# The second layer 23 pairs behind the first in place of 11, weights converted every third slot: attention and two gated layers on one core

## The chip, the cores and the metric

The kernel runs on one core of a Trainium2 chip. The metric is device time in microseconds (us) of one execution. Engines are named as the profile names them: PE (TensorE, matmuls), DVE (VectorE), ACT (ScalarE), POOL (GpSimd), SP (SyncE, which only issues DMAs).

## What is computed

The reference pools `kv` over 4x4 patches, projects it with `w_sr` to 768 keys that are values too, lets 12288 queries of width 128 attend to them, and sends the result through two layers (128 to 2048 to 128), each with an activation of its own:

```python
kv_flat = kv.reshape(B, H // 4, 4, W // 4, 4, C).mean(axis=(2, 4)).reshape(B, -1, C) @ w_sr
s = (q @ kv_flat.transpose(0, 2, 1)) / np.sqrt(C)
a = np.exp(s - s.max(-1, keepdims=True)); a /= a.sum(-1, keepdims=True) + 1e-09
x = a @ kv_flat
h = x @ moe_w_in                      # layer 1
x = (h * np.clip(h + 3.0, 0.0, 6.0) / 6.0) @ moe_w_out
h = x @ moe2_w_in                     # layer 2, beta = 1
g = np.where(h >= 1, h, np.where(h <= -1, 0.0, (h + 1) ** 2 / 4))
out = g @ moe2_w_out
```

## The kernel before, in words

All matrices are float32. To keep their accuracy a matrix is held as a high and a low part, and a product is made of three matmuls (high x high, high x low, low x high). The 12288 rows are cut into 24 blocks of 512. The 2048 hidden columns of a layer are cut into 16 pieces of 128, and two pieces make a **pair**. So each layer has 24 x 8 = 192 pairs, and pair `s` belongs to block `s // 8`.

The program is written out in **slots**, `T = 0, 1, 2, ...`, and each engine executes what it is given strictly in the order of the text, waiting where data or a buffer is not there. In slot `T` the function `slot` writes down pair `s1 = T` of layer 1 and pair `s2 = T - O2` of layer 2. O2 is the lag. So slots 0 to O2-1 have layer 1 alone, slots O2 to 191 have both layers, and slots 192 to 191+O2 have layer 2 alone.

What a pair does:

- **m_in** (L457): six matmuls of 512 columns into two tiles `h` of PSUM. There are four such tiles for both layers.
- Layer 1: `relu1` on ACT (L498, twice), `mul1` on DVE (L504, twice), then `hi_lo`: the high part on ACT (L532, twice), the low part on POOL (L533, twice).
- Layer 2: `clip2` on DVE (L511), `sq2` on ACT (L517), `max2` on DVE (L521), each twice, and `hi_lo` a slot later.
- **m_out** (L473): six matmuls that add the pair to `acc[m]`, one bank of PSUM for each layer. Layer 1's stand one slot later, layer 2's two slots later (`LAG2`), or three from slot `NS + LAG3_AT` on, where NS is 192. Layer 2's m_out stands last in a slot.
- After the eighth pair of a block layer 1's `acc[0]` is split into `x2h` (ACT, L480) and `x2l` (DVE, L481), the input of layer 2. Layer 2's `acc[1]` is transposed by DVE (`o_T`, L489) and stored. As there is one `acc[1]`, the first m_out of the next block waits for that transposition.

Attention for the next blocks lies between these. Four score tiles a block (`s_mm`, L364, six matmuls of 384 columns) are followed by the maximum on DVE (L375) and the exponential on ACT (L400). One slot later comes the tail: the sum's reciprocal on DVE (L408, L411), the product on ACT (L414, only while `T < ACT_T`), the low part on DVE (L421), and a transposing DMA. Twice a block `av` (L436, 18 matmuls of 256 columns) makes `xh` (ACT, L441) and `xl` (DVE, L442). From slot 4 on the score tiles stand in even slots and the tails in odd ones; in slots 0 to 4 every slot has scores. Queries are transposed by `q_T` (DVE L338, ACT L339, POOL L340).

The weights are **converted** when loaded, in 16 pieces `j0` to `j15` of 512 columns. A piece takes four steps, one a slot: step 0 is two ACT instructions (L163, L165); step 1 is two DVE instructions (L172, L174) and an addition on POOL (L176); step 2 is one DVE instruction (L181); step 3 is the high part on ACT (L192) and the low part on POOL (L194). They stand last but for the m_outs in a slot. Pieces 0 to 6 are begun ahead of slot 0; the slots in which 7 to 15 begin are listed in `CONV_AT`. A raw piece waits in a tile that another purpose leaves free (`stage`), and `LOADS` is the order of the loads.

Of the kernel before, what the change touches and what calls it, by code (L numbers as in the profile page):

```python
# [8 lines left out]
FP32 = mybir.dt.float32  # L9
F32R = mybir.dt.float32r  # L10
# [6 lines left out]
AX = mybir.AxisListType  # L17

W_MIN = 3.4332275390625e-05
O2, LAG2 = 11, 2  # L20

LOADS = "w k0 k1 w k4 k6 k2 k5 k3 w q0 k8 k7 k9 k10 k11 w w w w w q1 w w w w w w q2 w w"
KV_MODE = "DDVVPPPPPPPP"
PROLOGUE = """
j0.0 j0.1 k0 j1.0 k1 j0.2 k2 k3 g2 k4 g3 j1.1 t1 k5 j2.0 j0.3 p1 q0 k6 z1 t2 j2.1 p2 t0
# [3 lines left out]
j4.3 x1 j6.1 j5.3  # L32
"""
SPLIT0 = (0, 2)
CONV_AT = (0, 1, 4, 6, 7, 8, 10, 12, 14)
ACT_T = 32
LAG3_AT = 5
EARLY = (0, 1, 2, 3, 5, 7, 4, 6, 8, 10, 9, 13, 2)
EB = 3
AB = 3  # L40
SPLIT_AT = (5, 7, 9)
LO_DVE = ((0, 'out', 2),)
KV_ACT = (0, 1, 2, 3)

# [2 lines left out]
def tile_attn_moe_moe2(  # L47
# [18 lines left out]
    BLK = 512  # L66
# [9 lines left out]
    hl_p = ctx.enter_context(tc.tile_pool(name="hl", bufs=2))  # L76
    q_p = ctx.enter_context(tc.tile_pool(name="q", bufs=2))
    x_p = ctx.enter_context(tc.tile_pool(name="x", bufs=2))
    e_p = ctx.enter_context(tc.tile_pool(name="e", bufs=EB))
    a_p = ctx.enter_context(tc.tile_pool(name="a", bufs=AB))  # L80
    at_p = ctx.enter_context(tc.tile_pool(name="at", bufs=2))
# [18 lines left out]
    def f32(t):  # L100
        return t.bitcast(FP32)
# [4 lines left out]
    def new_h():  # L106
        return ps_h.tile([128, 512], FP32, tag="h", name="h")
# [76 lines left out]
    def w_stage3(job):  # L184
# [244 lines left out]
    def av(b, i, early=False):  # L429
        at = at_t.pop((b, i))  # L430
        ah, al = at[:, :KC], at[:, KC:]
        ps = (new_h() if early else new_s()[:, 0])[:, :BLK // 2]
        n = 0
        for k in range(KC):
            for l, r in ((vv[0], ah), (vv[0], al), (vv[1], ah)):
                nc.tensor.matmul(ps, l[:, k, :], r[:, k, :], start=(n == 0), stop=(n == 3 * KC - 1))  # L436
                n += 1
        if i == 0:
            x_t[b] = [x_p.tile([128, BLK], F32R, tag=f"x{p}", name=f"x{p}") for p in "hl"]
        hi, lo = (t[:, i * 256:(i + 1) * 256] for t in x_t[b])  # L440
# [19 lines left out]
    def m_out(m, s):  # L460
        b, c = divmod(s, NPAIR)
        assert (m, "out", c // 2) in ready
        if c == 0:
            acc[m] = ps_a.tile([128, BLK], FP32, tag=f"acc{m}", name=f"acc{m}")
        hi, lo = hl_t.pop((m, s))
        wh, wl = w_out[m]
        order = [(k, n) for k in range(2) for n in range(3)]
        if (m, s) == (1, NS - 1):
            order = [(0, 0), (0, 2), (1, 0), (1, 2), (0, 1), (1, 1)]
        for i, (k, n) in enumerate(order):  # L470
            ws = slice((2 * c + k) * 128, (2 * c + k + 1) * 128)
            l, r = ((wh, hi), (wh, lo), (wl, hi))[n]
            nc.tensor.matmul(  # L473
                acc[m], l[:, ws], r[:, k, :], start=(c == 0 and i == 0), stop=(c == NPAIR - 1 and i == 5)
            )
        if c == NPAIR - 1:
            if m == 0:
                hi = x_p.tile([128, BLK], F32R, tag="x2h", name="x2h")
                lo = x_p.tile([128, BLK], F32R, tag="x2l", name="x2l")
                nc.scalar.copy(out=hi, in_=acc[0])  # L480
                nc.vector.tensor_tensor(out=lo, in0=acc[0], in1=f32(hi), op=ALU.subtract)  # L481
                x2_t[b] = (hi, lo)
            else:
                o_t[b] = acc[1]
# [22 lines left out]

    def clip2(s, k):
        if k == 0:
            g_t[1, s] = hl_p.tile([128, 2, 512], FP32, tag="g2", name="g2")  # L510
        nc.vector.tensor_scalar(  # L511
            out=g_t[1, s][:, k], in0=h_t[1, s, k], scalar1=1.0, scalar2=-1.0, op0=ALU.min, op1=ALU.max
        )
# [8 lines left out]

    def hi_lo(m, s):
        g = g_t.pop((m, s))

        n = 1 if m == 0 or (s >= NS - O2 and s % 2) else 2
        hi = hl_p.tile([128, 2, 512], F32R, tag=f"h{n}", name=f"h{n}")
        lo = hl_p.tile([128, 2, 512], F32R, tag=f"l{n}", name=f"l{n}")
        hl_t[m, s] = hi, lo
        for k in range(2):  # L530
            eng = nc.vector if s == NS - 1 else nc.gpsimd
            nc.scalar.copy(out=hi[:, k], in_=g[:, k])  # L532
            eng.tensor_tensor(out=lo[:, k], in0=g[:, k], in1=f32(hi[:, k]), op=ALU.subtract)  # L533
# [3 lines left out]
    NS = NB * NPAIR  # L537
# [4 lines left out]
    s_at, tail_at, av_at, q_at, o_at = {}, {}, {}, {}, {}  # L542
# [39 lines left out]
    def slot(T):  # L582
        s1, s2 = T, T - O2
        if ok(s1):
            for k in range(2):
                m_in(0, s1, k)
                relu1(s1, k)
        if T in tail_at:
            s_tail_a(*tail_at[T], on_act=T < ACT_T)
            if T >= ACT_T:  # L590
                s_tail_b(*tail_at[T])
        if ok(s1):
            for k in range(2):
                mul1(s1, k)
        if ok(s2):
            for k in range(2):
                m_in(1, s2, k)
                clip2(s2, k)
        if ok(s2 - 1):
            hi_lo(1, s2 - 1)  # L600
        if ok(s1):
            hi_lo(0, s1)
        if T in o_at:
            o_T(o_at[T])
        if ok(s2):
            for k in range(2):
                sq2(s2, k)
        if T in s_at:
            s_mm(*s_at[T], split=T in SPLIT_AT)
        if T in tail_at and T < ACT_T:  # L610
            s_tail_b(*tail_at[T])
        if ok(s2):
            for k in range(2):
                max2(s2, k)
        if T in s_at:
            s_exp(*s_at[T])
        if T in av_at:
            av(*av_at[T], early=T < O2)
        if T in q_at:
            q_T(q_at[T])  # L620
        conv_step(T in CONV_AT)
        load_next()
        if ok(s1 - 1):
            m_out(0, s1 - 1)
        lag = LAG2 if T < NS + LAG3_AT else 3
        if ok(out2_at[0]) and s2 - lag == out2_at[0]:
            m_out(1, out2_at[0])
            out2_at[0] += 1
# [80 lines left out]
```

## Time and profile before

| | |
|---|---|
| median of 3 runs | 1354.13 us (1353.67 to 1357.67) |
| the profiled execution | 1357.25 us; its span, first to last instruction, 1355.5 us |
| busy | PE 1313.2 us (97%), DVE 1156.6 (85%), POOL 1079.2 (80%), ACT 1033.8 (76%) |
| mean granted clock of PE | 0.988 of full speed |

The profiled execution took 3.1 us more than the median of the runs, and 1.75 us of its time lie outside the span. Times of the trace count from the span's start. The granted clock is given as a share of 2.4 GHz; 0.5 is 1.2 GHz.

### The profile page before, as it was taken

The numbers are of one execution on the slowest core, as the hardware profiler recorded it, in microseconds if no ns is written. First come the engines' busy times: TensorE is split into PE (matmuls) and PEld (weight loads), VectorE is DVE, ScalarE is ACT, GpSimd is POOL, SyncE is SP. The second block draws the span as 40 slices with busy tenths as digits, with TensorE's granted clock in tenths as the row PEclk, the third lists the DMA queues.
The fourth block names the chain that finished last, engine by engine and source line by source line (L and its number), as shares of the span: only waits on it lengthen the run. The fifth ranks groups of instructions, "written<-read, shape, count | busy, mean of one in ns | idle before, by whom it ended". The sixth has DMA issues, their size and how long they took to land.

```text
span 1355.5 us, 18465 instructions
## 1 busy us (share of the span) xinstructions
PE 1313.2 (97%) x6244; PEld 1073.5 (79%) x6244; DVE 1156.6 (85%) x1815; ACT 1033.8 (76%) x1917; POOL 1079.2 (80%) x826
## 2 busy tenths in 40 slices
PE   8587999999999999999999999999999999999998
PEld 6465788888888888888888888888888888888876
DVE  3798988898988988888989989888898899898677
ACT  2678888877777787778777777877777777777776
POOL 2478998887887887888878878878878888787887
PEclk9789999999999999999999999999999999999999
DMA  9642221221212221212212122222212122121000
GB/s 326 130 93 39 59 46 33 47 40 36 51 32 43 40 43 34 49 33 43 47 28 52 32 43 41 43 43 40 43 32 51 32 44 34 33 43 25 8 9 16
DMA packets 260783, 66.28 MB, mean 49 GB/s; under 512 B 252368, under 2 KB 256592, under 8 KB 260688
## 3 DMA queue, kind: packets, MB, share of 16 engines
q1 hardware_dynamic: 259456, 62.94, 23.8%
q10 hardware_dynamic: 1232, 2.16, 0.4%
q8 instruction: 49, 0.80, 0.2%
q14 instruction: 46, 0.38, 0.1%
HBM read 21.04 MB, written 6.29 MB: 20 GB/s over the span
## 4 chain that ended last, share of the span: by engine, by line
PE 87%; DVE 4%; POOL 1%; ACT 1%; issue 1%; DMA 0%; ACTq 0%; DVEq 0%; POOLq 0%
PE acc L473 37%; PE h L457 37%; PE s L364 7%; PE s L436 6%; POOL l L533 1%; DVE t L504 1%; DVE a L421 1%; DVE nm L375 1%; DVE wa L172 0%; ACT t L498 0%; DVE g L181 0%; DVE wa L174 0%; DMA wst<-in_moe_w_out_dram 0%; ACT a L414 0%; DVE g L511 0%
## 5 line engine op out<-in xcount | busy, mean ns | idle before, releaser
L533 POOL TENSOR_TENSOR l<-g,h 128x512 fp32r<-128x512 f32 x382 | 507.9, 1351 | 210.0 <-ACT h L532 150.6
L533 POOL TENSOR_TENSOR l<-t,h 128x512 fp32r<-128x512 f32 x382 | 501.2, 1334 | 10.5 <-ACT h L532 7.1
L498 ACT ACTIVATE t<-h 128x512 f32<-128x512 f32 x384 | 227.1, 597 | 215.8 <-PE h L457 207.8
L504 DVE SCALAR_TENSOR_TENSOR t<-t,h 128x512 f32<-128x512 f32 x384 | 248.7, 682 | 128.2 <-ACT t L498 128.2
L521 DVE TENSOR_TENSOR g<-h,g 128x512 f32<-128x512 f32 x384 | 245.6, 679 | 13.4 <-ACT g L517 6.6
L532 ACT CAST h<-t 128x512 fp32r<-128x512 f32 x384 | 225.1, 620 | 35.2 <-DVE t L504 31.9
L511 DVE TENSOR_SCALAR g<-h 128x512 f32<-128x512 f32 x384 | 245.7, 680 | 0.7 <-POOL l L533 0.4
L517 ACT ACTIVATE g<-g 128x512 f32<-128x512 f32 x384 | 228.0, 628 | 1.7 <-DVE g L511 1.7
L532 ACT CAST h<-g 128x512 fp32r<-128x512 f32 x384 | 217.7, 617 | 4.2 <-DVE g L521 3.6
L457 PE MATMUL h<-xh,wi0h 128*128 128x512 f32 x384 | 152.6, 397 | 5.9 <-ACT xh L441 4.5
L473 PE MATMUL acc<-h,wo0h 128*128 128x512 f32 x384 | 156.2, 407 | 0.0
L473 PE MATMUL acc<-l,wo0h 128*128 128x512 f32 x384 | 153.1, 399 | 2.2 <-POOL l L533 2.0
L457 PE MATMUL h<-x2h,wi1h 128*128 128x512 f32 x384 | 152.4, 397 | 2.4 <-DVE g L521 2.2
L457 PE MATMUL h<-xl,wi0h 128*128 128x512 f32 x384 | 152.7, 398 | 0.7 <-DVE xl L442 0.7
L473 PE MATMUL acc<-h,wo1h 128*128 128x512 f32 x384 | 151.9, 396 | 0.5 <-DVE o L489 0.4
L457 PE MATMUL h<-x2h,wi1l 128*128 128x512 f32 x384 | 152.2, 396 | 0.0
L457 PE MATMUL h<-xh,wi0l 128*128 128x512 f32 x384 | 152.2, 396 | 0.0
L473 PE MATMUL acc<-h,wo0l 128*128 128x512 f32 x384 | 152.2, 396 | 0.0
L457 PE MATMUL h<-x2l,wi1h 128*128 128x512 f32 x384 | 151.7, 395 | 0.0
L473 PE MATMUL acc<-h,wo1l 128*128 128x512 f32 x384 | 151.3, 394 | 0.0
L473 PE MATMUL acc<-l,wo1h 128*128 128x512 f32 x384 | 151.3, 395 | 0.0
L421 DVE SCALAR_TENSOR_TENSOR a<-e,rc,a 128x768 f16<-128x768 f32 x96 | 137.2, 1429 | 3.3 <-ACT a L414 0.5
(134 smaller groups left out, 2128.6 us busy)
## 6 DMA issues: line engine op xcount, KB each, us to landing
q<-in_q_dram SPq DMA_DIRECT2D x96, 64.0 KB, 2.4
out_dram<-o SPq DMA_DIRECT2D x96, 64.0 KB, 1.9
h<-in_kv_dram SPq DMA_DIRECT2D x4, 512.0 KB, 8.9
l<-in_moe_w_in_dram SPq DMA_DIRECT2D x3, 512.0 KB, 8.7
at<-a SPq DMA_TRANSPOSE x96, 3.7
g<-in_moe_w_in_dram SPq DMA_DIRECT2D x2, 512.0 KB, 6.8
h<-in_moe_w_out_dram SPq DMA_DIRECT2D x2, 512.0 KB, 9.5
l<-in_kv_dram ACTq DMA_DIRECT2D x2, 512.0 KB, 10.4
```

Source lines behind the costliest of these rows:

```text
L364: nc.tensor.matmul(ps[h], l[:, js], r[:, ks], start=(n == 0), stop=(n == 2))
L421: nc.vector.scalar_tensor_tensor(out=a[:, 1], in0=e, scalar=rc, in1=a[:, 0], op0=ALU.mult, op1=ALU.subtract)
L436: nc.tensor.matmul(ps, l[:, k, :], r[:, k, :], start=(n == 0), stop=(n == 3 * KC - 1))
L457: nc.tensor.matmul(ps, l[:, ws], r, start=(n == 0), stop=(n == 2))
L473: nc.tensor.matmul(acc[m], l[:, ws], r[:, k, :], start=(c == 0 and i == 0), stop=(c == NPAIR - 1 and i == 5))
L498: nc.scalar.activation(out=g_t[0, s][:, k], in_=h_t[0, s, k], func=ACTF.Relu, scale=1.0 / 6.0, bias=0.5)
L504: nc.vector.scalar_tensor_tensor(out=g, in0=g, scalar=1.0, in1=h_t.pop((0, s, k)), op0=ALU.min, op1=ALU.mult)
L511: nc.vector.tensor_scalar(out=g_t[1, s][:, k], in0=h_t[1, s, k], scalar1=1.0, scalar2=-1.0, op0=ALU.min, op1=ALU.max)
L517: nc.scalar.activation(out=g, in_=g, func=ACTF.Square, scale=0.5, bias=0.5)
L521: nc.vector.tensor_tensor(out=g, in0=h_t.pop((1, s, k)), in1=g, op=ALU.max)
L532: nc.scalar.copy(out=hi[:, k], in_=g[:, k])
L533: eng.tensor_tensor(out=lo[:, k], in0=g[:, k], in1=f32(hi[:, k]), op=ALU.subtract)
```

## The change

O2 goes from 11 to 23. `CONV_AT` spaces the nine pieces by three slots (the first by two), so that at most one piece is in its DVE steps in any slot. Block inputs `x2h`, `x2l` get three buffers in place of two. In the slots with layer 2 alone, odd pairs take `t1`'s buffers for `g` and even ones their own. `LAG3_AT` goes from 5 to 17, so that a lag of three holds for the last six pairs as before. `ACT_T` goes from 32 to 26. The load of block 2's queries stands earlier. `EARLY_AV` keeps the choice of the PSUM tile of `av` as it was.

```diff
-O2, LAG2 = 11, 2
+O2, LAG2 = 23, 2
-LOADS = "w k0 k1 w k4 k6 k2 k5 k3 w q0 k8 k7 k9 k10 k11 w w w w w q1 w w w w w w q2 w w"
+LOADS = "w k0 k1 w k4 k6 k2 k5 k3 w q0 k8 k7 k9 k10 k11 w w w w w q1 w q2 w w w w w w w"
-CONV_AT = (0, 1, 4, 6, 7, 8, 10, 12, 14)
-ACT_T = 32
-LAG3_AT = 5
+CONV_AT = (0, 2, 5, 8, 11, 14, 17, 20, 23)
+ACT_T = 26
+LAG3_AT = O2 - 6
+EARLY_AV = 11
+    x2_p = ctx.enter_context(tc.tile_pool(name="x2", bufs=3))
-                hi = x_p.tile([128, BLK], F32R, tag="x2h", name="x2h")
-                lo = x_p.tile([128, BLK], F32R, tag="x2l", name="x2l")
+                hi = x2_p.tile([128, BLK], F32R, tag="x2h", name="x2h")
+                lo = x2_p.tile([128, BLK], F32R, tag="x2l", name="x2l")
-            g_t[1, s] = hl_p.tile([128, 2, 512], FP32, tag="g2", name="g2")
+            tag = "t1" if s >= NS - O2 and s % 2 else "g2"
+            g_t[1, s] = hl_p.tile([128, 2, 512], FP32, tag=tag, name=tag)
-            av(*av_at[T], early=T < O2)
+            av(*av_at[T], early=T < EARLY_AV)
```

Lines after L78 move by two or three, so DVE's L504 is L506 in the kernel of after, L172 is L174, and so on.

**DVE in slot 9 and up to slot 10's products.** Before, these are the products `t` of slot 9, the attention tail, and then step 2 of one piece and step 1 of the next ahead of slot 10's products:

```order
L504 SCALAR_TENSOR_TENSOR t_1029<-t_1029,h 128x512 x2
L421 SCALAR_TENSOR_TENSOR a<-e,rc,a 128x768
L442 SCALAR_TENSOR_TENSOR xl<-h,csc,xh 128x256
L181 SCALAR_TENSOR_TENSOR g_554<-g_554,wa 128x512
L172 TENSOR_SCALAR wa<-wa 128x512
L174 TENSOR_SCALAR wa<-wa 128x512
L504 SCALAR_TENSOR_TENSOR t_1092<-t_1092,h 128x512 x2
```

In the kernel of after the same slot reads:

```order
L506 SCALAR_TENSOR_TENSOR t_1021<-t_1021,h 128x512 x2
L423 SCALAR_TENSOR_TENSOR a<-e,rc,a 128x768
L444 SCALAR_TENSOR_TENSOR xl<-h,csc,xh 128x256
L174 TENSOR_SCALAR wa<-wa 128x512
L176 TENSOR_SCALAR wa<-wa 128x512
L506 SCALAR_TENSOR_TENSOR t_1081<-t_1081,h 128x512 x2
```

The step 2 (L181) of the other piece has left this slot; step 1 of one piece is still there.

**DVE in slots 11 and 12.** Before, layer 2 begins here with its clips (L511) and maxima (L521):

```order
L504 SCALAR_TENSOR_TENSOR t_1147<-t_1147,h 128x512 x2
L511 TENSOR_SCALAR g_1165<-h 128x512 x2
L421 SCALAR_TENSOR_TENSOR a<-e,rc,a 128x768
L521 TENSOR_TENSOR g_1165<-h,g_1165 128x512 x2
L172 TENSOR_SCALAR wa<-wa 128x512
L174 TENSOR_SCALAR wa<-wa 128x512
L504 SCALAR_TENSOR_TENSOR t_1201<-t_1201,h 128x512 x2
```

In the kernel of after slots 11 and 12, up to the products of slot 13, have layer 1 alone:

```order
L506 SCALAR_TENSOR_TENSOR t_1130<-t_1130,h 128x512 x2
L423 SCALAR_TENSOR_TENSOR a<-e,rc,a 128x768
L506 SCALAR_TENSOR_TENSOR t_1168<-t_1168,h 128x512 x2
L377 TENSOR_REDUCE nm<-s 128x1
L174 TENSOR_SCALAR wa<-wa 128x512
L176 TENSOR_SCALAR wa<-wa 128x512
L410 TENSOR_SCALAR su<-su 128x1
L413 RECIPROCAL rc<-su 128x1
L506 SCALAR_TENSOR_TENSOR t_1208<-t_1208,h 128x512 x2
```

Layer 2's instructions have left the slot, and step 1 of a piece now stands behind the maximum of a slot with scores.

**PE at the end of a block of layer 2, in slots with layer 2 alone.** Before, this happens once, in slot 197, where the lag goes from two to three: the m_in rows of slots 197 and 198 (twelve L457, of which eleven are shown) stand ahead of the first m_out into the next `acc`:

```order
L457 MATMUL h<-x2l,wi1h 128x512
L457 MATMUL h<-x2h,wi1l 128x512
L457 MATMUL h<-x2h,wi1h 128x512
L457 MATMUL h<-x2l,wi1h 128x512
L457 MATMUL h<-x2h,wi1l 128x512
L457 MATMUL h<-x2h,wi1h 128x512
L457 MATMUL h<-x2l,wi1h 128x512
L457 MATMUL h<-x2h,wi1l 128x512
L457 MATMUL h<-x2h,wi1h 128x512
L457 MATMUL h<-x2l,wi1h 128x512
L457 MATMUL h<-x2h,wi1l 128x512
L473 MATMUL acc_13827<-h_13763,wo1h 128x512
```

In the kernel of after it happens in slots 193, 201 and 209. Slot 209 looks like the rows above. In slot 201, as in 193, six matmuls stand between the last of one `acc` and the first of the next:

```order
L475 MATMUL acc_13363<-h_13516,wo1l 128x512
L459 MATMUL h<-x2h,wi1h 128x512
L459 MATMUL h<-x2l,wi1h 128x512
L459 MATMUL h<-x2h,wi1l 128x512
L459 MATMUL h<-x2h,wi1h 128x512
L459 MATMUL h<-x2l,wi1h 128x512
L459 MATMUL h<-x2h,wi1l 128x512
L475 MATMUL acc_13586<-h_13543,wo1h 128x512
L475 MATMUL acc_13586<-l_13544,wo1h 128x512
```

On DVE the transposition of `acc_13363` stands behind the clips of those six matmuls' results:

```order
L525 TENSOR_TENSOR t_13536<-h,t_13536 128x512 x2
L515 TENSOR_SCALAR g_13563<-h 128x512 x2
L491 STREAM_TRANSPOSE o<-acc_13363 128x512
L525 TENSOR_TENSOR g_13563<-h,g_13563 128x512 x2
L515 TENSOR_SCALAR t_13597<-h 128x512 x2
```

The transposition has not moved within its slot; what moved is the slot, from one with two layers to one with layer 2 alone.

## Rows read from the trace of the kernel before

**Rows 1.** Busy time in three stretches: from slot 0, from slot 13, layer 2 alone.

```profile
60.80:139.30 78.50, 64.83 (x270) 50.30 (x271) 69.99 (x98) 60.67 (x110) 63.24 (x44) 0.89 0.39 81
139.30:1314.80 1175.50, 1174.28 (x5569) 962.94 (x5568) 1022.06 (x1600) 918.63 (x1703) 970.31 (x742) 1.00 0.21 38
1314.80:1350.30 35.50, 35.37 (x151) 27.94 (x149) 32.65 (x52) 28.07 (x47) 28.40 (x23) 1.00 0.05 9
```

**Rows 2.** PE in order of time, slots 5 and 6: start, duration, instruction.

```profile
92.38 0.39 PE L436 MATMUL h<-at,vh 128*128 128x256 f16 x2
...
94.28 0.48 PE L473 MATMUL acc<-h,wo0h 128*128 128x512 f32 x1
...
95.76 0.39 PE L457 MATMUL h<-xh,wi0h 128*128 128x512 f32 x1
...
97.17 0.34 PE L364 MATMUL s<-kTh,qh 128*128 128x384 f32 x1
...
98.22 0.39 PE L473 MATMUL acc<-h,wo0h 128*128 128x512 f32 x1
```

**Rows 3.** ACT in order of time, slots 5 and 10.

```profile
94.04 1.07 ACT L498 ACTIVATE t<-h 128x512 f32<-128x512 f32 x2
...
96.86 0.48 ACT L441 ACTIVATE xh<-h,csc 128x256 fp32r<-128x256 f32 x1
97.22 1.08 ACT L498 ACTIVATE t<-h 128x512 f32<-128x512 f32 x2
...
125.53 0.90 ACT L400 ACTIVATE e<-s,nm 128x768 f32<-128x768 f32 x1 [0.25 <-DVE nm L375]
...
126.42 0.61 ACT L339 CAST qh<-qT 128x512 fp32r<-128x512 f32 x1
...
127.48 0.66 ACT L163 ACTIVATE wa<-wst 128x512 f32<-128x512 f32 x1
...
128.60 1.06 ACT L498 ACTIVATE t<-h 128x512 f32<-128x512 f32 x2
```

**Rows 4.** DVE in order of time, end of slot 9 and slot 10.

```profile
120.47 1.51 DVE L172 TENSOR_SCALAR wa<-wa 128x512 f32<-128x512 f32 x1
...
123.36 1.27 DVE L504 SCALAR_TENSOR_TENSOR t<-t,h 128x512 f32<-128x512 f32 x2
124.55 0.94 DVE L375 TENSOR_REDUCE nm<-s 128x1 f32<-128x768 f32 x1
```

**Rows 5.** DVE groups from 62 to 142 us: count, busy us, mean ns.

```profile
L172 DVE TENSOR_SCALAR wa<-wa 128x512 f32<-128x512 f32 x8 | 9.6, 1201 | 0.0
L174 DVE TENSOR_SCALAR wa<-wa 128x512 uint32<-128x512 uint32 x8 | 7.3, 918 | 0.3
L181 DVE SCALAR_TENSOR_TENSOR l<-l,wa 128x512 uint32<-128x512 uint32 x2 | 2.5, 1257 | 0.0
```

**Rows 6.** The same groups from 30 to 52 us, ahead of slot 0.

```profile
L174 DVE TENSOR_SCALAR wa<-wa 128x512 uint32<-128x512 uint32 x2 | 0.9, 428 | 0.1
L172 DVE TENSOR_SCALAR wa<-wa 128x512 f32<-128x512 f32 x2 | 0.8, 410 | 0.0
L181 DVE SCALAR_TENSOR_TENSOR l<-l,wa 128x512 uint32<-128x512 uint32 x1 | 0.7, 693 | 0.0
```

**Rows 7.** PE in order of time, from the end of slot 197's m_in.

```profile
1331.62 0.40 PE L457 MATMUL h<-x2h,wi1h 128*128 128x512 f32 x1
...
1333.29 0.47 PE L473 MATMUL acc<-h,wo1h 128*128 128x512 f32 x1
```

**Rows 8.** DVE at the same place.

```profile
1332.43 0.70 DVE L489 STREAM_TRANSPOSE o<-acc 128x512 f32<-128x512 f32 x1
```

**Rows 9.** PE in order of time, two idle times and matmuls behind them.

```profile
107.32 0.61 PE L457 MATMUL h<-xh,wi0h 128*128 128x512 f32 x1 [2.20 <-ACT xh L441]
...
110.14 0.52 PE L364 MATMUL s<-kTh,qh 128*128 128x384 f32 x1
...
129.96 0.50 PE L457 MATMUL h<-xh,wi0h 128*128 128x512 f32 x1 [1.34 <-DVE t L504]
```

## The prediction

> **What bounds the kernel now.** I read first the busy time by stretches. The reader is to see that PE works without a gap from slot 13 on: 1174.28 of 1175.50 us, and 35.37 of 35.50 in the slots with layer 2 alone, both at full clock [rows 1]. Between the first m_in of slot 0 (60.80 us) and that of slot 13 (139.30 us) it is busy for only 64.83 of 78.50 us, at a granted clock of 0.89. The number of matmuls doesn't change, so the time can only change where PE idles or is slow: in the ramp, and wherever the change opens a new gap.
>
> How much does the ramp lose? PE in order of time at full clock gives the prices: `av` 1.90 us (92.38 to 94.28), six matmuls of m_in 1.41 (95.76 to 97.17), a score tile 1.05 (97.17 to 98.22) [rows 2]. I count 1.41 for m_out too. Up to slot 13 PE has 13 m_ins and 12 m_outs of layer 1, two m_ins of layer 2, 9 score tiles and 3 `av`: 27 x 1.41 + 9 x 1.05 + 3 x 1.90 = 53.2 us. So 78.5 - 53.2 = 25.3 us are lost. The change can gain at most that, and it puts twelve more slots with layer 1 alone in the ramp, whose own losses come out of the gain.
>
> **What sets the length of a ramp slot.** Not PE, but the chain between ACT and DVE. In a slot with scores, DVE makes the products (123.36), then the maximum (124.55); ACT starts the exponential at 125.53 [rows 3, 4] and is free for the next thing at 126.42, 3.06 us after the products began. Then comes what else ACT has: a query cast and step 3 of a piece, together 1.06 (126.42 to 127.48), step 0 1.12 (127.48 to 128.60) [rows 3], and then the next relu, 0.63 us ahead of the next products (relu pairs and product pairs are each about 1.2 us long and overlap by half). So such a slot takes 3.06 + 0.63 = 3.69 us and ACT's extras. A slot with a tail and `av` takes 3.18 us of ACT (relu at 94.04 to relu at 97.22 [rows 3]) and extras; without `av` and its cast (96.86 to 97.22) 2.82. The rule gives slot 10 of before as 123.36 - 0.63 + 3.69 + 1.06 + 1.12 = 128.60, which is where the relu of slot 11 stands.
>
> DVE adds pushes: steps 1 and 2 stand ahead of the next products. At the end of slot 9 the two instructions of step 1 took from 120.47 to 123.36, 2.89 us [rows 4], while ACT had written slot 10's relu long before. In the ramp L172 and L174 take 1.20 and 0.92 us in the mean, L181 1.26 [rows 5]; ahead of slot 0, where POOL has little to do, the first three take 0.41, 0.43 and 0.69 [rows 6]. So step 1 costs 2.1 us in the ramp against 0.84, and step 2 1.2 against 0.7. The Trainium skill ("SBUF — State Buffer", section "SBUF: two separate sides") says why: DVE and POOL share a pair of ports under an exclusive lock, and the loser waits for the other's whole instruction. The trace agrees with it (0.41 against 1.20 us), and it speaks against the change: spacing the pieces makes none of them cheaper as long as POOL is fed in every slot.
>
> **The change part by part.**
>
> *Ahead of slot 0 and slots 0 to 4: about 0.2 us gained.* On DVE and ACT the same instructions stand in the same order ahead of slot 0; the earlier query load meets an SP queue with nothing to issue. Slots 0 to 4 hold two steps 1 as before and a step 2 in slot 4. I take relu of slot 5 at 93.8 in place of 94.04.
>
> *Slots 5 to 10.* Two pieces in place of four have their steps 1 here. Slots with steps 3 and 0 (0.53 + 1.12 us of ACT): slot 5 3.18 + 1.65 = 4.9, slot 8 3.69 + 1.65 = 5.4 and 0.8 for the cast to `x2h` (0.5) and PE's wait for `xh`, which stands there today [rows 9] (0.3 of it reaches ACT, by choice), 6.2. Slots with step 1: slot 6, where DVE is free 2.78 us after relu, then 2.1 and 0.35 for the reciprocal, so the products come 0.9 late, 4.7; slot 9, where tail and `xl` last until 3.6 and step 1 until 5.7 against products due at 3.8, 5.2. Slots with step 2: slot 7 4.5, slot 10 3.69 + 0.53, 4.3 with a little push. Sum 29.8 us against 34.6 before (94.04 to 128.60 [rows 3]). Relu of slot 11 stands at 123.6, 5.0 us earlier.
>
> *Slots 11 to 22.* Scores and tails alternate, so the same rules hold. Slots 11, 14, 17, 20 with steps 3 and 0: 4.5 + 5.4 + 4.9 + 5.4 = 20.2. Slots 12, 15, 18, 21 with step 1, pushed by 1.0 to 2.0 us: 4.7 + 4.4 + 5.2 + 5.1 = 19.4 (18 has the query cast). Slots 13, 16, 19, 22 with step 2: 4.2 + 4.2 + 3.4 + 3.7 = 15.5. Sum 55.1 us, 4.6 a slot, where PE needs 24 x 1.41 + 6 x 1.05 + 3 x 1.90 = 45.8. Relu of slot 23 stands at 178.7.
>
> *Layer 2's begin.* Before, from relu of slot 11 (128.60) to m_in of slot 13 (139.30) 10.7 us pass. Slots 23 and 24 hold the same work without the step 1 that pushed slot 12's products (2.1 us), and with the copies to `x2h` and `x2l` that fall in slot 24, two of the casts' 0.53: 10.7 - 2.1 + 1.1 = 9.7. So m_in of slot 25 starts at 188.4.
>
> *Balance of the ramp: 3.3 us lost.* Up to slot 25 after, PE has 24 half slots, 6 score tiles and 3 `av` more than up to slot 13 before, 45.8 us. With no change in losses slot 25 would begin at 139.30 + 45.8 = 185.1; it begins at 188.4. Bounds: if steps 1 and 2 cost what they cost beside an idle POOL [rows 6], the pushes of slots 6 to 22 shrink by 3 x 1.0 (even slots, whole push) + 3 x 1.26 (odd) + 3 x 0.5 (step 2), 8 us, so 5 gained; if each of the six steps 1 costs 2.89 [rows 4], 5 more, so 8 lost.
>
> *The end: 3.3 us lost.* When a block of layer 2 ends, PE's next m_out waits until DVE has transposed `acc[1]`, and the transposition stands behind two clips that need this slot's m_in. Before, that happens among slots with layer 2 alone once, in slot 197, and there the lag rises to three, so that PE has m_in of slot 198 to do first. Its m_in of slot 197 ends at 1331.62, the transposition runs from 1332.43 for 0.70 us, and m_out starts at 1333.29 [rows 7, 8]. Without the m_in between, PE would have idled for 1333.29 - 1331.62 = 1.67 us. After, blocks end in slots 193, 201 and 209; only 209 has the lag of three. So two waits of 1.67 us each, 3.3. Behind them all of PE's remaining work is queued, and PE has no slack there. A bound below is nothing if DVE ran ahead of PE; it can't, as the clips need this slot's m_in.
>
> *Nothing.* The third `x2` buffer, the alternating `g` buffers and ACT_T change no instruction's length, and behind slot 26 PE covers the other engines as it does now: none is busy for more than 83% (POOL 970.31 of 1175.50 us [rows 1]). Without that cover ACT_T would put three products more on DVE, in slots 27, 29 and 31, each below 1.3 us by the rows of DVE at hand.
>
> *The clock.* Behind PE's idle time of 2.20 us at 107.32 the next m_in took until 110.14, 2.82 us in place of 1.41: the clock was at the lower level, and the score matmul at 110.14 still took 0.52 us against 0.34 at 97.17 [rows 2, 9]. Behind 1.34 us of idle time at 129.96 nothing of the kind shows. The two new waits of 1.67 us lie between. They stand in dense work, like that at 129.96, and the nearer row is 1.34, so I take nothing; a fall would cost the 1.4 us of that m_in and a little of what follows, 1.7 by choice, so up to 3.4 for both.
>
> Sum: 3.3 + 3.3 = 6.6 us slower. Against the profiled execution's 1357.25 that is 1363.9; it ran 3.1 above the median of 1354.13, so a median of **1360.7**.
>
> **The rivals.**
>
> *The ramp runs at PE's pace (faster).* If POOL, with one piece in three slots, leaves DVE the gaps it needs, the pushes vanish: slots 5 to 22 take 76.9 in place of 84.9 us and the median is 1352.7; down to PE's own 71.7 us there (25.9 and 45.8) it is 1347.5. It decides from a step 1 near 0.84 us on. For it: POOL gets fewer instructions per slot. Against it: the means of [rows 5] were taken while POOL idled for a fifth of the time (63.24 of 78.50 us busy [rows 1]). 22%, three quarters of it below 1350.
>
> *The gains and losses cancel.* The ramp gains 0 to 4, with slots that I made too long (PE may run ahead of ACT by the four `h` tiles, which smooths some pushes), the end loses 3.3: 1353.4 to 1357.4. 22%.
>
> *A low clock in the longer ramp.* Each slot of 11 to 22 leaves PE 0.8 us idle, in one piece if it waits for one instruction. If the clock falls there as at 107.32, PE itself becomes the limit: three to five falls of 1.7 us, 1365.8 to 1369.2. Against it: 0.8 is below the 1.34 that brought no fall. 12%.
>
> *Forecast, 1357 to 1365.* 44%. That the change doesn't do what it says is ruled out by the order of instructions above.
>
> **How the numbers follow.** About 0.3% (4 us) is what the runs can tell from no change, so faster is below 1350.1 and slower above 1358.2. Faster takes three quarters of the first rival, 0.17; same its rest, the second rival and the lower edge of the forecast, 0.32; slower the remainder, 0.51. The range of 1350 to 1369 leaves out 2 in 10, mostly below. The forecast's own range is 1357 to 1365.
>
> **What would show it.** The first layer 2 m_in near 180 us; slots 11 to 22 of 4.6 us each, with PE idle 0.8 a slot and its waits named after DVE's products or ACT; L172 and L174 at a mean of 2 us together; two waits of PE's m_out for the transposition, of 1.67 us, some 70 and 46 us ahead of the end (slots of 2.8 us). It is wrong if step 1 falls to 1 us, if slots 11 to 22 come near 3.9 us, or if the two waits are absent.

## The result: slower by 0.7%

The kernel of after takes 1364.72 us in the median of 4 runs (1363.41 to 1366.01), the kernel before 1354.06 us on the same chip (4 runs, 1353.67 to 1357.67). The ratio is 1.0073, with an interval of 1.0053 to 1.0092. The forecast was 1360.7 us, slower, in a range of 1350 to 1369.

A median of 4 runs of the kernel before can lie 2 to 3 us low: in later comparisons, with 17 to 35 runs, its median was 1355.97 to 1356.92 us, and after is 7.8 to 8.8 us (about 0.6%) slower than that. So I judge the steps by the two profiled executions, 1357.25 us before and 1364.46 us after: 7.2 us slower, where the sum of the prediction was 6.6.

The head of the page of after: the span and the busy time of each engine.

```profile
span 1362.6 us, 18443 instructions
...
PE 1313.9 (96%) x6244; PEld 1070.3 (79%) x6244; DVE 1160.5 (85%) x1818; ACT 1035.6 (76%) x1914; POOL 1077.3 (79%) x826
```

PE is busy for 0.7 us more than before (1313.2 us), so 6.4 of the 7.1 us of the span are idle time of PE. The busy time by stretches shows where it lies. As in [rows 1], a row gives the stretch and its length, then the busy time (and the instructions) of PE, PEld (PE's loading of weights), DVE, ACT and POOL, then the granted clock, the busy share of the DMA engines and GB/s. The stretches are slots 0 to 4, 5 to 10 and 11 to 22 (counted from relu to relu), then up to the m_in of slot 25, the long middle, and the first 49 us of the end.

```profile
61.20:91.98 30.78, 25.80 (x110) 20.36 (x110) 28.32 (x39) 23.08 (x43) 23.50 (x17) 0.89 0.45 104
91.98:123.18 31.20, 26.94 (x130) 19.79 (x129) 24.42 (x39) 24.15 (x47) 23.63 (x17) 1.00 0.41 83
123.18:179.30 56.12, 48.45 (x236) 37.88 (x236) 44.03 (x64) 45.46 (x84) 47.72 (x35) 1.00 0.28 52
179.30:188.51 9.21, 7.50 (x34) 5.77 (x33) 8.66 (x15) 9.21 (x20) 7.87 (x6) 1.00 0.22 43
188.51:1290.00 1101.49, 1099.56 (x5213) 902.40 (x5212) 962.12 (x1503) 853.12 (x1583) 900.57 (x692) 1.00 0.21 38
1290.00:1339.00 49.00, 46.00 (x197) 36.66 (x196) 44.02 (x68) 39.56 (x65) 41.25 (x33) 1.00 0.07 11
```

The m_in of slot 25 starts at 188.51. The ramp without change in losses would have had it at 185.1, so 3.4 us are lost there. The middle has 1.93 us of PE's idle time against 1.22 behind slot 13 before [rows 1], 0.7 more. The end has 3.0 us of idle time, and 0.17 us more at each of its two waits, as worked out below. These make 3.4 + 0.7 + 3.3 = 7.4 us, against 7.1 measured.

**The ramp.** PE's waits from 91 to 190 us (who was waited for, us in total, times, longest):

```profile
PE acc L475 <- POOL l L536: 7.4, 11, 1.2
...
PE h L459 <- DVE g L525: 1.7, 1, 1.7
```

PE mostly waits for POOL's low part of the products, yet POOL is busy for 47.72 of 56.12 us in slots 11 to 22 and isn't short of time. The low part is the last link. ACT and DVE in order of time at the begin of slot 16, where step 1 of a piece stands behind slot 15's tail, show the first one:

```profile
144.32 1.10 ACT L500 ACTIVATE t<-h 128x512 f32<-128x512 f32 x2
144.38 1.49 DVE L174 TENSOR_SCALAR wa<-wa 128x512 f32<-128x512 f32 x1
...
145.90 1.39 DVE L176 TENSOR_SCALAR wa<-wa 128x512 uint32<-128x512 uint32 x1
...
147.21 1.27 DVE L506 SCALAR_TENSOR_TENSOR t<-t,h 128x512 f32<-128x512 f32 x2
...
147.92 1.22 ACT L535 CAST h<-t 128x512 fp32r<-128x512 f32 x2 [2.51 <-DVE t L506]
```

The relu begins at 144.32, but DVE is in step 1 from 144.38 to 147.2, the products follow at 147.21, and ACT has idled for 2.51 us when it makes their high part. So the products were pushed by more than 2 us, and everything behind them with them. The groups of step 1 on DVE from 62 to 190 us have these means:

```profile
L176 DVE TENSOR_SCALAR wa<-wa 128x512 uint32<-128x512 uint32 x9 | 11.6, 1288 | 0.3
...
L174 DVE TENSOR_SCALAR wa<-wa 128x512 f32<-128x512 f32 x10 | 9.5, 952 | 0.0
```

Together 2.24 us, against 2.12 in the kernel before (1.20 + 0.92 [rows 5]): the first became cheaper and the second dearer, and spacing the pieces made step 1 as a whole no cheaper.

**Where layer 2 begins.** PE in order of time in slot 12 of before, from layer 2's m_in to the m_in of slot 13:

```profile
133.83 0.50 PE L457 MATMUL h<-x2h,wi1h 128*128 128x512 f32 x1 [2.23 <-DVE g L521]
...
135.24 0.63 PE L457 MATMUL h<-x2h,wi1l 128*128 128x512 f32 x1
...
139.30 0.39 PE L457 MATMUL h<-xh,wi0h 128*128 128x512 f32 x1
```

The same matmuls in slot 24 of after, up to the m_in of slot 25:

```profile
184.54 0.51 PE L459 MATMUL h<-x2h,wi1h 128*128 128x512 f32 x1 [1.71 <-DVE g L525]
...
188.51 0.40 PE L459 MATMUL h<-xh,wi0h 128*128 128x512 f32 x1
```

In between PE works without a wait in both kernels, for 5.47 us before and 3.97 after. Before, the granted clock is 0.64 from 133.5 to 138.3: behind 2.23 us of idle time it fell to the lower level (1.2 GHz), and a matmul of 512 columns is shown with 0.63 us in place of 0.39. After, it stays at 1.00 behind 1.71 us of idle time. Up to these m_ins both kernels take the same, 5.23 us from relu of slot 11 (128.60 to 133.83) and 5.24 from relu of slot 23 (179.30 to 184.54). So the 1.5 us that after gains where layer 2 begins are a fall of the clock that it doesn't have.

**The end.** DVE and PE in order of time in slot 193, the first of the two places where a block of layer 2 ends with layer 2 alone:

```profile
1290.20 1.32 DVE L515 TENSOR_SCALAR g<-h 128x512 f32<-128x512 f32 x2
...
1290.39 0.40 PE L459 MATMUL h<-x2h,wi1l 128*128 128x512 f32 x1
...
1291.44 0.71 DVE L491 STREAM_TRANSPOSE o<-acc 128x512 f32<-128x512 f32 x1
...
1292.29 0.47 PE L475 MATMUL acc<-h,wo1h 128*128 128x512 f32 x1 [1.50 <-ACT g L521]
```

The last matmul of m_in starts at 1290.39; in a dense stretch the next starts 0.23 us later, at 1290.62, but m_out starts at 1292.29, 1.67 us late, of which 1.50 are shown as idle. The second place, at 1316.43, has the same 1.50. The row names ACT's square as the releaser, which ended at about the same time as the transposition; that it is the transposition is shown by the experiment below that moves it.

### The profile page after: what moved, and what is told of

Its sections match the earlier page's. It is cut to its first block, busy times and chain, and to the rows that moved or that the text cites. A ratio compares the mean times of both kernels' runs of the same rounds, so it can differ in the third digit from the quotient of the medians.

```text
span 1362.6 us, 18443 instructions
## 1 busy us (share of the span) xinstructions
PE 1313.9 (96%) x6244; PEld 1070.3 (79%) x6244; DVE 1160.5 (85%) x1818; ACT 1035.6 (76%) x1914; POOL 1077.3 (79%) x826
## 4 chain that ended last, share of the span: by engine, by line
PE 78%; DVE 6%; ACT 3%; issue 1%; POOL 0%; DVEq 0%; ACTq 0%
PE acc L475 34%; PE h L459 33%; PE s L366 6%; PE s L438 6%; DVE g L525 1%; DVE g L515 1%; DVE t L506 1%; DVE t L525 1%; ACT g L521 1%; ACT h L535 1%; ACT t L521 0%; ACT t L500 0%; DVE t L515 0%; DVE nm L377 0%; POOL l L536 0%
## 5 line engine op out<-in xcount | busy, mean ns | idle before, releaser
L536 POOL TENSOR_TENSOR l<-g,h 128x512 fp32r<-128x512 f32 x360 | 472.0, 1332 | 204.3 <-ACT h L535 153.0
L536 POOL TENSOR_TENSOR l<-t,h 128x512 fp32r<-128x512 f32 x404 | 533.8, 1342 | 25.7 <-ACT h L535 23.3
L506 DVE SCALAR_TENSOR_TENSOR t<-t,h 128x512 f32<-128x512 f32 x384 | 248.2, 682 | 120.9 <-ACT t L500 120.7
L535 ACT CAST h<-t 128x512 fp32r<-128x512 f32 x408 | 240.0, 620 | 40.1 <-DVE t L506 33.2
L525 DVE TENSOR_TENSOR g<-h,g 128x512 f32<-128x512 f32 x360 | 230.6, 681 | 13.6 <-ACT g L521 7.1
L515 DVE TENSOR_SCALAR g<-h 128x512 f32<-128x512 f32 x360 | 230.9, 682 | 0.7
L521 ACT ACTIVATE g<-g 128x512 f32<-128x512 f32 x360 | 214.7, 629 | 1.5 <-DVE g L515 1.1
L535 ACT CAST h<-g 128x512 fp32r<-128x512 f32 x360 | 204.2, 617 | 5.2 <-DVE g L525 5.2
## 6 DMA issues: line engine op xcount, KB each, us to landing
l<-in_kv_dram ACTq DMA_DIRECT2D x2, 512.0 KB, 10.3
```

The lines of the kernel that those rows point to most:

```text
L506: nc.vector.scalar_tensor_tensor(out=g, in0=g, scalar=1.0, in1=h_t.pop((0, s, k)), op0=ALU.min, op1=ALU.mult)
L515: nc.vector.tensor_scalar(out=g_t[1, s][:, k], in0=h_t[1, s, k], scalar1=1.0, scalar2=-1.0, op0=ALU.min, op1=ALU.max)
L521: nc.scalar.activation(out=g, in_=g, func=ACTF.Square, scale=0.5, bias=0.5)
L525: nc.vector.tensor_tensor(out=g, in0=h_t.pop((1, s, k)), in1=g, op=ALU.max)
```

## The experiments

Theory: after loses about 3.3 us where step 1 and step 2 push the products in the long ramp, and 3.3 at the end behind two transpositions. Rivals: the first profile of before was not typical; the loss is the clock's; or the ramp is slow for a reason other than DVE's steps. "Before" in a ratio is always the kernel before on the same chip and in the same comparison.

### The kernel before again

> The kernel before, unchanged, for a profile of an execution nearer to its median than the one shown (1357.25 against 1354.06 us). Every theory: ratio 1.000. If the executions of before differ in the prologue or the ramp, this trace has its first m_in of slot 0 or of slot 13 earlier than 60.80 and 139.30 us by up to 3 us; if they differ in the matmul rate, both stay and the stretch from slot 13 to the end is shorter.

No edit. 1356.71 us (12 runs) against 1356.92 (35 runs), ratio 0.9984 (0.9967 to 1.0000). The profile has a span of 1355.7 us, its first m_in at 61.02 and the waits of the first one. So the profiled execution of before was a typical one, and the low median of the first runs was the exception.

### After, transposition ahead of the clips at the end

> The kernel after, with the transposition of layer 2's finished block ahead of the clips in slots with layer 2 alone. Theory of two losses (ramp, and two waits of PE for the transposition at the end): the two waits of 1.50 us with 0.17 us of drain each go, 3.3 us, so 1361.4 us against 1364.7. Rival, ramp alone (the waits only take the place of waits that PE would have there anyway): 1364.7 us, the idle time shows up at another instruction of PE.

```diff
+        if T in o_at and T >= NS:
+            o_T(o_at[T])
         if ok(s2):
             for k in range(2):
                 m_in(1, s2, k)
                 clip2(s2, k)
...
-        if T in o_at:
+        if T in o_at and T < NS:
             o_T(o_at[T])
```

1361.60 us (12 runs), ratio 1.0026 (1.0010 to 1.0043), 3.1 us below after. PE's waits from 1270 us on are now this one row; of the two of 1.50 us nothing is left:

```profile
PE acc L475 <- DVE o L491: 0.2, 1, 0.2
```

The 3.1 us compare medians of two comparisons, in which before differed by 2.9 us; the traces settle it. From relu of slot 25 to the span's end after takes 1172.32 us (190.28 to 1362.6) and this kernel 1169.17 (191.13 to 1360.3), 3.15 less. The loss at the end is shown, and its size too (3.3 predicted).

### Before, the lag of three one pair later

> The kernel before, with the lag of three from slot 198 on in place of 197, so that a block of layer 2 ends in a slot with layer 2 alone and a lag of two. Theory of two losses: one wait of PE of 1.5 us for the transposition appears some 23 us ahead of the end, 1.7 us slower, 1355.7 us. Rival, ramp alone: no such wait or no cost, 1354.1 us.

```diff
-LAG3_AT = 5
+LAG3_AT = 6
```

1358.00 us (12 runs), ratio 1.0005 (0.9986 to 1.0024): in time no more than the scatter, so that the 1.7 us expected are neither shown nor refuted. The trace of this kernel has, among PE's waits from 1270 us on, the one new wait that was expected, named after ACT's square as in after:

```profile
PE acc L473 <- ACT g L517: 1.5, 1, 1.5
```

So what hides the transposition in the kernel before is the m_in that the longer lag puts in front of m_out.

### After without DVE's part in the conversion of pieces 9 to 15

> The kernel after without the three DVE instructions of the conversion in pieces 9 to 15 (steps 1 and 2; the rest of a piece stays; layer 2's weights are then wrong). Theory of pushes: the products of a slot no longer wait for them, slots 5 to 22 shrink by 8 us as in the lower bound of the prediction's ramp, 1357 us, and the mean slot from 11 to 22 falls from 4.7 to 4.2 us. Rival, ACT's own work and PE set the slots and DVE's steps are hidden: at most 2 us faster, 1363 us or more.

The two instructions of step 1 and the one of step 2 on DVE are left out for these pieces, so that the weights of layer 2 but one piece are wrong.

```diff
 def w_stage1(job):
     a, r = wcv[job]
+    if w_jobs.index(job) >= 9:
+        nc.gpsimd.tensor_tensor(out=a.bitcast(I32), in0=a.bitcast(I32), in1=r, op=ALU.add)
+        return
...
 def w_stage2(job):
     a, r = wcv.pop(job)
+    if w_jobs.index(job) >= 9:
+        return
```

1354.46 us (12 runs), ratio 0.9966 (0.9948 to 0.9985), 10.3 us below after; 8 were expected. The addition on POOL stays. The relus of slots 5, 11 and 23, ACT in order of time:

```profile
92.37 1.07 ACT L505 ACTIVATE t<-h 128x512 f32<-128x512 f32 x2
...
120.91 1.09 ACT L505 ACTIVATE t<-h 128x512 f32<-128x512 f32 x2
...
171.58 0.60 ACT L505 ACTIVATE t<-h 128x512 f32<-128x512 f32 x1
```

Slots 11 to 22 take 50.7 us in place of 56.1, 4.2 each, and slots 5 to 10 take 28.5 in place of 31.2: 8.1 us together, as expected. The whole span is 9.5 us shorter (1353.1). So the pushes are DVE's steps, and cost 1.4 to 1.5 us for each of the seven pieces. The run shows more: without any push these slots still take 4.2 us where PE's own work is 45.8 / 12 = 3.8, and the change makes twelve more of them. What sets these 4.2 us is likely the chain through ACT: ACT is busy for 45.66 of the 50.67 us, and POOL, busy for 46.51, waits for ACT's high part when it idles. No run tries this.

### After with steps 1 in slots with scores, and in slots with tails

> The kernel after with pieces begun in slots 0, 1, 3, 5, ... 15, one in two slots from slot 1 on. Step 1 (two DVE instructions) then always falls in a slot with scores, where DVE has until the exponential and the next relu are through, and steps 0 and 2 in one with a tail. Theory of pushes (a piece costs what its DVE steps push the next products): a pair of slots takes 8.5 us with a piece in place of 9.2 and more, slots 5 to 22 shrink from 87 to 77 to 80 us, 1355 to 1358 us against 1364.7. Rival, the number of pieces in flight sets the cost: twice as dense is worse than every third slot in slots 5 to 18 and gives it back in 19 to 22, 1364 us or more.

> As e5, but begun in slots 0, 2, 4, ... 16, so that step 1 always falls in a slot with a tail (up to slot 18). The same spacing. Theory of pushes: a pair of slots takes 9.2 to 9.9 us, slots 5 to 22 take 83 to 86 us, so 3 to 7 us slower than e5: 1361 to 1363 us. Rival, number in flight: the same as e5 within 1.5 us.

```diff
-CONV_AT = (0, 2, 5, 8, 11, 14, 17, 20, 23)
+CONV_AT = (0, 1, 3, 5, 7, 9, 11, 13, 15)
```

```diff
-CONV_AT = (0, 2, 5, 8, 11, 14, 17, 20, 23)
+CONV_AT = (0, 2, 4, 6, 8, 10, 12, 14, 16)
```

Odd starts, whose step 1 stands in even slots (scores): 1360.20 us (6 runs), ratio 1.0036 (1.0024 to 1.0049). Even starts, with step 1 in odd slots (tails): 1365.21 us (5 runs), ratio 1.0067 (1.0055 to 1.0079). Both begin a piece every second slot, so the number of pieces in work is the same; the kind of slot is worth 5.0 us, in the expected 3 to 7, and the rival (the same within 1.5 us) is out. Both times themselves were missed, each by 2.2 us: 1355 to 1358 and 1361 to 1363 were expected. DVE with odd starts, products of slots 13, 14 and 15:

```profile
131.22 0.91 DVE L174 TENSOR_SCALAR wa<-wa 128x512 f32<-128x512 f32 x1
132.16 1.40 DVE L176 TENSOR_SCALAR wa<-wa 128x512 uint32<-128x512 uint32 x1
...
133.75 1.26 DVE L506 SCALAR_TENSOR_TENSOR t<-t,h 128x512 f32<-128x512 f32 x2
...
138.43 1.27 DVE L506 SCALAR_TENSOR_TENSOR t<-t,h 128x512 f32<-128x512 f32 x2
...
143.03 1.27 DVE L506 SCALAR_TENSOR_TENSOR t<-t,h 128x512 f32<-128x512 f32 x2
```

The same with even starts:

```profile
134.08 1.28 DVE L506 SCALAR_TENSOR_TENSOR t<-t,h 128x512 f32<-128x512 f32 x2 [0.29 <-ACT t L500]
...
137.20 0.65 DVE L174 TENSOR_SCALAR wa<-wa 128x512 f32<-128x512 f32 x1
137.88 1.40 DVE L176 TENSOR_SCALAR wa<-wa 128x512 uint32<-128x512 uint32 x1
139.20 1.27 DVE L506 SCALAR_TENSOR_TENSOR t<-t,h 128x512 f32<-128x512 f32 x2
...
144.00 1.28 DVE L506 SCALAR_TENSOR_TENSOR t<-t,h 128x512 f32<-128x512 f32 x2 [0.27 <-ACT t L500]
```

Two slots take 9.28 us with odd starts (133.75 to 143.03), where 8.5 was expected, and 9.92 with even ones (134.08 to 144.00). Between the two kernels steps 0, 2 and 3 change their kind of slot, too. The kernel of after, which has both kinds, and the one without DVE's steps price step 1 by itself. Products of slots 9 and 10 in after:

```profile
114.61 1.26 DVE L506 SCALAR_TENSOR_TENSOR t<-t,h 128x512 f32<-128x512 f32 x2
...
119.60 1.27 DVE L506 SCALAR_TENSOR_TENSOR t<-t,h 128x512 f32<-128x512 f32 x2
```

The same without DVE's steps:

```profile
114.29 1.27 DVE L511 SCALAR_TENSOR_TENSOR t<-t,h 128x512 f32<-128x512 f32 x2
...
117.32 1.28 DVE L511 SCALAR_TENSOR_TENSOR t<-t,h 128x512 f32<-128x512 f32 x2
```

With step 1 behind a tail, slot 9 takes 4.99 us from products to products in place of 3.03, and slot 15 takes 5.07 in place of 2.83. With step 1 in a slot with scores, slots 6 and 12 take 4.58 and 4.64 in place of 3.70. So step 1 pushes by 2.0 to 2.2 us in the one kind and by 0.9 in the other (in slots 21 and 18 by 1.0 and 0.5). In a slot with scores a part of it fills the time in which ACT makes the exponential and DVE would wait for its sum anyway. In a slot with a tail it stands behind the tail's low part, with the next products due. After uses both kinds in turn and lies between: from relu of slot 0 to relu of slot 25 the traces take 125.20 us with odd starts, 127.78 in after and 130.20 with even ones. Its median (1364.72 against 1365.21 with even starts) doesn't show this difference, and why is open.

### Before with odd starts

> The kernel before with pieces begun in slots 0, 1, 3, 5, ... 15 in place of 0, 1, 4, 6, 7, 8, 10, 12, 14: the lag stays at 11. Theory of pushes: slots 5 to 10 shrink from 34.6 to 29 or 30 us, some of it is lost again where layer 2 begins, 3 to 5 us faster than before, 1352 to 1354 us against 1356.9. Rival, number in flight or lag alone: within 1.5 us of before.

```diff
-CONV_AT = (0, 1, 4, 6, 7, 8, 10, 12, 14)
+CONV_AT = (0, 1, 3, 5, 7, 9, 11, 13, 15)
```

1354.04 us (11 runs) against 1356.42, ratio 0.9986 (0.9977 to 0.9994): faster than the kernel before, by 2.4 us where 3 to 5 were expected. Slots 5 to 10 take 30.4 us (92.81 to 123.23) in place of 34.6; a part is lost behind them, where PE waits 2.2 us for layer 2's low weights (`wi1l`, at 166.57). It is the fastest kernel of this study.

### A lag of 17

> The kernel after with a lag of 17 in place of 23 and pieces begun in slots 0, 2, 4, 6, 8, 11, 13, 15, 17. Theory of two losses: six slots with layer 1 alone fewer, so half of the ramp's loss; a block of layer 2 ends in slot 195, not covered, and in 203, covered by the lag of three, so one wait of 1.5 us at the end in place of two: 1359 to 1361 us. Rival, ramp alone: 1360 to 1362 us without a change in the waits at the end.

```diff
-O2, LAG2 = 23, 2
+O2, LAG2 = 17, 2
-CONV_AT = (0, 2, 5, 8, 11, 14, 17, 20, 23)
+CONV_AT = (0, 2, 4, 6, 8, 11, 13, 15, 17)
```

1422.62 us (5 runs), ratio 1.0500 (1.0486 to 1.0514), where 1359 to 1361 was expected. PE is busy for 1329.4 us, and its longest waits are these:

```profile
PE acc L475 <- DVE o L491: 47.1, 21, 2.4
```

PE and DVE in order of time at one of the 21 places:

```profile
334.04 1.27 DVE L506 SCALAR_TENSOR_TENSOR t<-t,h 128x512 f32<-128x512 f32 x2
334.42 0.39 PE L475 MATMUL acc<-h,wo0l 128*128 128x512 f32 x1
...
335.24 1.28 DVE L515 TENSOR_SCALAR g<-h 128x512 f32<-128x512 f32 x2
...
336.44 0.70 DVE L491 STREAM_TRANSPOSE o<-acc 128x512 f32<-128x512 f32 x1
...
337.19 0.50 PE L475 MATMUL acc<-h,wo1h 128*128 128x512 f32 x1 [2.38 <-DVE o L491]
```

It is the wait of the end, now in every block. The block of layer 2 whose output is transposed ends in slot 8b + 26 with this lag, so that the transposition and the next block's first m_out stand in slot 8b + 27. Slots 3 and 7 of eight have neither scores nor `av`, so that PE has only two m_ins and layer 1's m_out to do before, and idles for 2.38 us until DVE is through. With lags of 11 and 23 the place is slot 8b + 21 or 8b + 33, which have an `av`. The expectation had counted the ramp and the end and overlooked the phase. The sum: 47.1 us of waits, and PE busy 15.5 us longer than in after (1329.4 against 1313.9) at a lower clock; without both the span of 1422.7 would be 1360.1.

### A lag of 15; a lag of 17 with the transposition first

> The kernel of after with a lag of 15 and the starts 0, 1, 3, 5, 7, 9, 11, 13, 15. Theory (what cost the lag of 17 its 62 us is where the last pair of a block of layer 2 falls: with 17 the next block's first m_out stands in slots 8b+27, which have neither score tiles nor av, so that PE reaches it ahead of the transposition): with 15 these are slots 8b+25, which have an av, as with 11 and 23; no wait for o in the slots with both layers, one of 1.5 us in the slots with layer 2 alone, and a time between the kernels of lag 11 and lag 23 with such starts: 1354.0 + 4/12 x (1360.2 - 3.3 - 1354.0) + 1.7 = 1356.7. Rival (a lag between 11 and 23 costs time for another reason, such as the buffers of the block input): over 1380.

> The lag of 17 with the transposition written ahead of the clips in every slot. The same theory: the transposition, which began at 336.44 behind the clips' 1.28 us, begins some 1.2 us earlier, so that each of the 21 waits of 2.38 us falls to about 1.2; a wait of 1.2 us brought no low clock so far, so the ten low clocks (15.5 us of PE) go too: 1422.6 - 21 x 1.2 - 15.5 = 1382. If the low clock were not the waits' doing, 1397; if the waits were not the transposition's, 1422.

```diff
-O2, LAG2 = 17, 2
+O2, LAG2 = 15, 2
-CONV_AT = (0, 2, 4, 6, 8, 11, 13, 15, 17)
+CONV_AT = (0, 1, 3, 5, 7, 9, 11, 13, 15)
```

The second one has the lag of 17, and `o_T` ahead of `clip2` as above but in every slot.

The lag of 15: 1356.63 us (12 runs), ratio 0.9997 (0.9985 to 1.0009), as expected to 0.1 us, which is closer than the runs can tell (1352.79 to 1359.19). Between 200 and 1300 us PE's waits are one row, in place of 46.6 us for the lag of 17:

```profile
PE acc L475 <- DVE o L491: 0.4, 1, 0.4
```

The lag of 17 with the transposition first: 1382.26 us (4 runs), ratio 1.0198 (1.0185 to 1.0211); 1382 was expected. Each wait is 1.18 us now, since the transposition begins where the clips did:

```profile
220.37 0.70 DVE L491 STREAM_TRANSPOSE o<-acc 128x512 f32<-128x512 f32 x1
...
221.13 0.50 PE L475 MATMUL acc<-h,wo1h 128*128 128x512 f32 x1 [1.18 <-DVE o L491]
```

Its PE is busy for 1311.7 us, and the granted clock is 1.00 behind each of these waits. Both runs show that the phase of the block's end, and no cost of a middle lag, made the 1422 us.

### After with odd starts and the transposition first

> The kernel of after with odd starts and the transposition ahead of the clips in slots with layer 2 alone: if the two gains are separate they add up, 1360.2 - 3.1 = 1357.1, as far from the kernel before as a measurement can tell; if odd starts only moved the waits, 1360 or more.

Both edits together: 1357.08 us (11 runs) against 1355.97, ratio 1.0006 (0.9995 to 1.0016). The two gains add up (1357.1 expected). With both losses mended, the long lag is level with the kernel before, and 3.0 us slower than the lag of 11 with odd starts (1354.04; by the ratios of the two comparisons, 1.0006 and 0.9986, 2.7 us).

### Before with odd, earlier starts

> The kernel before with starts 0, 1, 2, 3, 5, 7, 9, 11, 13: odd as in the earlier run with 1354.0, but each piece from the third one slot earlier or more, so that PE's wait of 2.2 us for layer 2's low weights (wi1l) goes. If that wait was on the path, 1352; if more pieces in slots 2 to 5 push the exponentials, 1355 or more.

```diff
-CONV_AT = (0, 1, 4, 6, 7, 8, 10, 12, 14)
+CONV_AT = (0, 1, 2, 3, 5, 7, 9, 11, 13)
```

1356.95 us (11 runs), ratio 1.0004 (0.9992 to 1.0016): a miss, since 1352 was expected if that wait was on the path; the other branch, 1355 or more, came. The wait for `wi1l` is gone, but DVE's query transposition in an early slot waits for its DMA:

```profile
82.31 0.71 DVE L338 STREAM_TRANSPOSE qT<-q 128x512 f32<-128x512 f32 x1 [3.03 <-DMA q<-in_q_dram]
```

In the run with 1354.04 it stands at 79.7. The conversion frees tiles earlier, so that weights are asked for earlier; that these loads are what delays the queries is likely, but wasn't tried by itself.

## Why the prediction was right

The sign, the two places and their sizes hold, and the chain of step 1, products and relu is the one described. The ramp's sum came out to 0.1 us because three errors of 0.5 to 1.0 us cancelled, and that is luck; one term was right for a wrong reason. The terms are measured here from products to products (L506). The relu doesn't serve in slot 5, since there it ran 2.56 us ahead of its products, which a step 2 on DVE held up. ACT and DVE of after:

```profile
91.98 1.07 ACT L500 ACTIVATE t<-h 128x512 f32<-128x512 f32 x2
...
94.54 1.26 DVE L506 SCALAR_TENSOR_TENSOR t<-t,h 128x512 f32<-128x512 f32 x2
```

The products of slot 5 before:

```profile
94.66 1.28 DVE L504 SCALAR_TENSOR_TENSOR t<-t,h 128x512 f32<-128x512 f32 x2 [1.31 <-ACT t L498]
```

- *Slots 0 to 4.* Predicted a gain of 0.2 us; the products of slot 5 stand at 94.54 in place of 94.66, 0.1 gained. Slot 1 no longer has step 0 of a second piece, which I overlooked, and the products of slot 2 are 0.9 us earlier (75.20 against 76.14), but by slot 5 this is used up.
- *Slots 5 to 10.* Predicted 29.8 us, measured 29.3 (94.54 to 123.81). The pushes of slots 6 and 9 were put at 0.9 and 1.9 us; against the kernel without DVE's steps they are 0.9 and 2.0.
- *Slots 11 to 22.* Predicted 55.1 us, 4.6 a slot; measured 56.1 (123.81 to 179.93). The largest miss is slot 19, 4.64 us in place of 3.4: a step 2 behind a tail, put at a small push, cost 1.6 (3.00 without DVE's steps). PE idles for 7.67 us in the twelve slots, 0.64 a slot; 0.8 was forecast.
- *Layer 2's begin.* Predicted 9.7 us; 9.2 measured (179.30 to 188.51), against 10.7 before. The reason was wrong: I took the gain from a step 1 that no longer pushes, but up to layer 2's m_in nothing is gained, and the 1.5 us are the fall of the clock behind 2.23 us of idle time that before has there and that I had not seen. The first m_in of layer 2 stands at 178.34, near 180 as forecast.
- *The ramp's balance.* With +0.1 - 0.5 + 1.0 - 0.5 = +0.1 the m_in of slot 25 stands at 188.51 in place of 188.4.
- *The price of step 1.* 2.1 us predicted, 2.24 measured; that these steps push the products is shown by leaving them out. The Trainium skill ("SBUF — State Buffer", section "SBUF: two separate sides") calls the pair of ports that DVE and POOL share an exclusive lock, which one of them holds for a whole instruction. The trace agrees: at 144.38 L174 takes 1.49 us and ends 0.28 behind a low part on POOL (144.00 to 145.59), and at 159.14, where one is just ending (159.17), it takes 0.38.
- *The names of the waits.* Forecast after DVE's products or ACT; they are named after POOL's low part (11 waits, 7.4 us). The chain is the one described, but its last link is POOL's, and this I had not seen.
- *The end.* Two waits of 1.67 us, 70 and 46 us ahead of the span's end (1292.29 and 1316.43 of 1362.6): right in place and in size.
- *Nothing.* The middle lost 0.7 us that I had put at nothing. 1.2 us of its waits stand at 208.82 and 211.41, behind slot 27, where ACT_T puts the first product on DVE (L418 at 204.94, 1.26 us); that this made them was not tried. That no engine is busy for more than 83% there was misread: DVE is busy for 1022.06 of 1175.50 us, 87% [rows 1].
- *The clock.* No fall behind the waits of 1.50 us (1.00 from 1290 to 1339), and 1.00 in slots 5 to 22: the rival of a low clock in the longer ramp didn't happen. The first rival (faster) failed on its own condition, since step 1 didn't get cheaper; the second because the ramp didn't gain.
- *The conversion to the median* made most of the distance from 1360.7 to 1364.72: 1363.9 was the sum for a profiled execution and 1364.46 came. I took off 3.1 us because the profile lay above the median of three runs, but these runs were the low ones.

## What to carry to other kernels

A longer lag between two pipelined layers makes more slots with one layer alone, and costs time if these run slower than the engine that bounds the rest. Here they took 4.2 us with all pushes gone, where PE needs 3.8, so lags of 11, 15 and 23 with odd starts gave 1354.0, 1356.6 (one wait of 1.67 at its end included) and 1357.1 us (no such wait). Before changing a lag, look at the slot in which each block's single accumulator is read out, and at what the bounding engine has to do meanwhile: 17 in place of 15 or 23 cost some 60 us by that alone, in waits and in the falls of the clock behind them. And where work must be slipped into an engine's fixed order, choose the slot in which that engine would wait anyway: this gave 5 us between two kernels with the same spacing, and a step 1 cost 0.9 us in the one kind of slot and 2.0 to 2.2 in the other.

## What the hardware showed that I had not expected

With the lag of 17 the waits of 2.38 us brought a lower clock behind them, but only at 9 places out of 19 (the other two of the 21 waits are shorter), mostly at every second block. Busy time of that kernel in two stretches, up to and behind the end of the wait at 280.13 (the granted clock is the third number from the right):

```profile
279.00:281.00 2.00, 0.87 (x4) 0.74 (x5) 2.00 (x4) 1.11 (x2) 2.00 (x3) 1.00 0.67 123
281.00:285.00 4.00, 4.00 (x12) 3.13 (x11) 0.94 (x2) 1.17 (x3) 0.91 (x1) 0.58 0.38 65
```

At 337.19 the same wait, with the same work around it, brought no fall. Behind a fall the next of these waits comes 57.06 us later (280.13 to 337.19) and without one 55.51 (337.19 to 392.70), so a fall cost 1.55 us, near the 1.50 at layer 2's begin in the kernel before. Waits of 1.18, 1.50 and 1.71 us brought none. In the ramp, waits of 2.20 us [rows 9] and 2.23 brought one in the kernel before, and with the lag of 11 and odd starts one of 2.13, at 128.76, brought none (1.00). Why it is one in two is open.
